# Packing one head group's q projection into pad rows, gathering it over DRAM, and laying the instruction order anew

## The chip, the cores and the metric

The kernel runs on one core of a Trainium2 chip. The metric is device time in microseconds (us), the median of several executions. The trace gives a span that is some 1.8 us shorter (182.2 us of span is 183.97 us of time in the profiled run of the kernel before). Ratios below are the mean time of one kernel's fast runs over that of the other's fast runs of the same rounds, so they are not quite the ratios of the medians that are quoted. "Clock" is the granted clock of TensorE in the records, 1.00 being full.

The kernel before was run again beside every experiment on the same chip. Its medians then lay between 184.4 and 185.2 us, single executions between 184.0 and 187.0 (and one of 441, an outlier), so differences under 0.3% are read with care. The record marks an execution as slow when it is over 1.5% above the fastest of the same kernel; such executions are left out of every ratio quoted here.

## The reference

Two branches are mixed by a gate for each token. S = 2048 tokens, D = 448, H = 16 heads of 28, four segments of 512 tokens, F = 1792.

```
g = sigmoid(sum(x * gate_w))
q, k, v = heads(x @ wq), heads(x @ wk), heads(x @ wv)
for s in 4 segments:                               # attention with a compressive memory
    a_dot = softmax(causal(q_s k_s^T / sqrt(28))) v_s
    a_mem = phi(q_s) M / (phi(q_s) z + 1e-6)       # phi(t) = t+1 if t>0 else exp(t)
    o_s   = sigmoid(beta) * a_mem + (1 - sigmoid(beta)) * a_dot
    M, z += phi(k_s)^T v_s, sum phi(k_s)
a = o @ wo
b = (gelu(layernorm(x)^T @ w1 + b1) @ w2 + b2)^T   # mixes tokens: w1 is 2048 x 1792
out = g * a + (1 - g) * b
```

## The kernel before

All five engines follow one fixed list of steps, `PLAN`. Each entry names a step and its engine (`@P` TensorE, `@A` ScalarE, `@D` VectorE, `@G` GpSimd, `@S` SyncE, which issues DMAs); digits after it are buffers. Each engine works through its own entries strictly in this order and waits on semaphores for the others. So the list decides what TensorE does while ScalarE works on exponentials.

Four heads of 28 form a group of 128 partitions, each head with four pad rows. A k/q projection is a `pair`: k in the lower, q in the upper half of the array, 14 matmuls. With four groups (`hg`) and four token chunks (`tc`) there are 16 pairs:

```
def pair(eng, u, tc, hg):
    ...
        for i in range(7):
            for h, c, bb in ((0, LC[i], bk), (1, UC[i], bq)):
                last = e.matmul(bank(bb)[:, 0:512], wkq[half[h], c, 128*hg : 128*hg+128],
                                xTb[half[h], b, i, :], start=(i == 0), stop=(i == 6), ...)
def ek(...): copy k out of its PSUM bank        # eviction; eq the same for q
def sc(...): scores of one of five groups of tiles of two head groups   (TensorE)
def exp(...): exponential of 128x2048           (ScalarE)
def mask(...): causal mask                      (GpSimd)
def pv(...): P times V                          (TensorE)
def ta, tm, nr, oa, om, oo, ot: normalize one of 16 items, memory and local part  (VectorE)
def mm_u, eu / mm_y, fin: the two MLP products and their evictions / last additions
```

Part of the list around 46 us, which this document comes back to: the pair of the last head group of chunk 2 stands between two score groups.

```
... u.2.7@P mask.1.2@G u.2.8@P ot.1@D sc.1.3@P ek.2.2@A
pair.2.3@P01 xtc.3@S oa.0@D1 exp.1.3@A2 ot.0@D ldr.2@S2 pv.2@P31 eq.2.3@D ek.2.3@A mask.1.3@G sc.1.4@P ...
```

The softmax here doesn't subtract the row's maximum and nothing guards it: scores larger than these inputs give would overflow.

Of the kernel before, what the change touches and what calls it, by code (L numbers as in the profile page):

```python
# [4 lines left out]
ALU = mybir.AluOpType  # L5
# [16 lines left out]
NO = 3  # L22
# [11 lines left out]
warm@P ldwk.0@A dve0@D id@G ldx.0@S ldx.1@S ldwq.0@A setup@G ldsm@S ldwv.0@A ldwv.1@A acttab@A ldwk.1@S ldwq.1@S  # L34
trx.0.2@P xw.0@D xtd.1@S trx.0.3@P trx.0.0@P trx.0.1@P trx.0.6@P trx.0.4@P trx.0.5@P trx.1.2@P xw.1@D trx.1.3@P
trx.1.0@P trx.1.1@P ex.1@A trx.1.6@P trx.1.4@P ex.0@D trx.1.5@P ex.2@D ex.3@A pad.0@D tb@A bn.3@D pair.0.0@P01 bn.0@D
bet@D btr@P2 eq.0.0@A ek.0.0@A pair.0.1@P31 b2c@D pad.1@A gcp@D b1c@D bn.1@D bn.2@D sc.0.0@P xtc.1@S v.1@P02 ek.0.1@D
lnc.0@G exp.0.0@A0 eq.0.1@D ldx.2@S pkm.0.0@D0 pair.0.3@P31 ldr.0@S0 ev.2@D pke.0.0@A0 ev.3@D sc.0.1@P gt.1@A
pkn.0.0@D eq.0.3@A pair.0.2@P02 exp.0.1@A1 ek.0.3@D pair.1.0@P13 ldx.3@S bn.5@D eq.0.2@A bn.4@D mask.0.0@G xtd.2@S
ek.0.2@A lna.0@D mask.0.1@G sc.0.2@P lna.1@A bn.6@D pair.1.3@P20 eq.1.0@A pkm.0.1@D1 lna.2@A bn.7@D pke.0.1@A1  # L40
ek.1.0@D lnc.1@G eq.1.3@D pair.1.1@P31 exp.0.2@A2 ek.1.3@D pkn.0.1@D v.3@P02 lna.3@D eq.1.1@A bn.11@D ek.1.1@A bn.9@D
sc.0.3@P mask.0.2@G ev.6@A v.0@P13 ev.7@D ldx.4@S lna.4@A bn.10@D gt.3@A exp.0.3@A3 pkt.0.0@S0 bn.8@D pair.1.2@P02
ev.0@D lnc.2@G ev.1@D pkt.0.2@S lna.7@A lna.6@D sc.0.4@P gt.0@A ek.1.2@D eq.1.2@A pv.0@P10 lna.5@A bn.15@D xtc.2@S
v.2@P32 exp.0.4@A0 pqm.1.1@D0 bn.14@D ldr.1@S1 bn.12@D mask.0.3@G u.0.0@P0 bn.13@D u.0.1@P u.0.2@P ev.5@A u.0.3@P
mask.0.4@G gc.0@D u.0.4@P ev.4@A u.0.5@P lna.8@D u.0.6@P u.0.7@P lna.9@A sc.1.0@P pqm.1.0@D1 lnc.3@G u.0.8@P pkt.0.3@S
gt.2@A lna.10@D pqe.1.1@A0 u.0.9@P u.1.0@P2 gc.1@D u.1.1@P u.1.2@P lna.11@D u.1.3@P pqe.1.0@A1 pv.1@P31 pqn.1.1@D
pkt.0.1@S u.0.10@P exp.1.0@A1 ta.0@D u.0.11@P u.1.4@P u.1.5@P pqn.1.0@D u.1.6@P u.1.7@P xtd.3@S u.1.8@P u.1.9@P
pkm.1.0@D1 u.1.10@P u.1.11@P lna.15@D lna.12@A sc.1.1@P mask.1.0@G nr.0@D lna.14@A mst.0@P1 pkm.1.1@D0 lna.13@D
exp.1.1@A5 ta.1@D u.1.12@P u.1.13@P u.1.14@P msa.0@D u.1.15@P u.0.12@P u.0.13@P eu.1@D u.0.14@P pke.1.1@A0 mask.1.1@G
sc.1.2@P nr.1@D pair.2.2@P31 msc.0@D pke.1.0@A1 oa.1@D0 exp.1.2@A0 pkn.1.1@D u.2.0@P2 u.2.1@P u.2.2@P pkn.1.0@D  # L50
u.2.3@P ldwo@S u.0.15@P u.2.4@P u.2.5@P eu.0@D u.2.6@P eq.2.2@A u.2.7@P mask.1.2@G u.2.8@P ot.1@D sc.1.3@P ek.2.2@A
pair.2.3@P01 xtc.3@S oa.0@D1 exp.1.3@A2 ot.0@D ldr.2@S2 pv.2@P31 eq.2.3@D ek.2.3@A mask.1.3@G sc.1.4@P ta.2@D u.3.0@P1
exp.1.4@A3 mem.4@P00 u.2.9@P pqm.2.1@D2 mem.5@P31 tm.4@D u.2.10@P pkt.1.0@S1 u.2.11@P u.2.12@P u.2.13@P tm.5@D
u.2.14@P u.2.15@P pqe.2.1@A0 u.3.1@P nr.2@D mask.1.4@G u.3.2@P eu.2@D sc.2.0@P pkt.1.1@S pair.3.3@P03 oa.2@D2
exp.2.0@A1 pqn.2.1@D ldr.3@S0 ot.2@D pv.3@P20 ek.3.3@A eq.3.3@D mask.2.0@G sc.2.1@P u.3.3@P ta.3@D exp.2.1@A5 u.4.0@P0
u.3.4@P u.4.1@P pkt.1.2@S pkm.2.1@D1 u.4.2@P u.4.3@P nr.3@D u.4.4@P u.3.5@P oa.3@D0 u.3.6@P v.7@P32 pke.2.1@A1
mask.2.1@G pkt.1.3@S ot.3@D pkn.2.1@D sc.2.2@P ev.15@A u.3.7@P u.3.8@P ev.14@D exp.2.2@A0 u.3.9@P u.3.10@P u.3.11@P
u.3.12@P u.3.13@P u.3.14@P u.3.15@P u.4.5@P u.4.6@P eu.3@D ldr.4@S1 gt.7@A u.4.7@P mask.2.2@G u.4.8@P u.4.9@P wo.0@P20
u.5.0@P3 u.5.1@P ea.0@A u.5.2@P u.5.3@P wo.1@P11 wo.2@P22 ea.1@D sc.2.3@P ea.2@A pv.4@P11 exp.2.3@A2 u.4.10@P ta.4@D
u.4.11@P u.4.12@P u.4.13@P u.4.14@P nr.4@D u.4.15@P v.6@P21 eu.4@D mask.2.3@G oa.4@D1 sc.2.4@P om.4@D ev.13@A wo.3@P03  # L60
exp.2.4@A3 ev.12@D u.5.4@P oo.4@D u.5.5@P u.5.6@P ea.3@D u.5.7@P u.5.8@P u.5.9@P u.5.10@P ot.4@D gt.6@A u.5.11@P
mask.2.4@G u.5.12@P u.5.13@P gc.3@D u.5.14@P u.5.15@P pair.3.2@P01 eu.5@A ldr.5@S2 pv.5@P20 eq.3.2@A mem.6@P30
ek.3.2@A pqm.3.1@D3 mst.1@P1 ta.5@D pqe.3.1@A0 tm.6@D sc.3.0@P v.5@P02 exp.3.0@A1 nr.5@D msa.1@D oa.5@D2 u.6.0@P3
u.6.1@P u.6.2@P ev.10@D u.6.3@P mask.3.0@G sc.3.1@P om.5@D u.6.4@P exp.3.1@A5 u.6.5@P u.6.6@P ev.11@D mem.7@P11
u.6.7@P oo.5@D u.6.8@P u.6.9@P tm.7@D u.6.10@P u.6.11@P u.6.12@P gt.5@A u.6.13@P pqn.3.1@D mask.3.1@G sc.3.2@P v.4@P10
exp.3.2@A0 msc.1@D ot.5@D u.6.14@P ev.8@D u.6.15@P u.7.0@P2 u.7.1@P eu.6@A mask.3.2@G ev.9@D sc.3.3@P u.7.2@P gelu.0@A
u.8.0@P3 u.8.1@P u.8.2@P u.8.3@P u.8.4@P u.8.5@P u.8.6@P u.8.7@P u.8.8@P u.8.9@P u.8.10@P u.8.11@P u.8.12@P u.8.13@P
u.8.14@P u.8.15@P u.7.3@P u.7.4@P eu.8@D u.7.5@P u.7.6@P u.7.7@P u.7.8@P pv.6@P31 u.7.9@P ta.6@D u.7.10@P u.7.11@P
gt.4@A exp.3.3@A2 u.7.12@P gc.2@D pair.3.0@P01 nr.6@D oa.6@D0 u.7.13@P mask.3.3@G om.6@D eq.3.0@A u.7.14@P u.7.15@P
sc.3.4@P ek.3.0@A eu.7@D ldr.6@S0 pair.2.0@P31 exp.3.4@A3 oo.6@D ot.6@D pair.2.1@P02 ek.2.0@D eq.2.0@A mask.3.4@G  # L70
sc.4.0@P ek.2.1@A eq.2.1@D pv.7@P30 exp.4.0@A1 pkm.2.0@D0 pair.3.1@P10 ta.7@D pqm.2.0@D1 nr.7@D pke.2.0@A1 u.9.0@P2
mask.4.0@G eq.3.1@D u.10.0@P3 u.10.1@P u.10.2@P oa.7@D1 u.10.3@P pqe.2.0@A0 u.10.4@P u.10.5@P u.9.1@P pqm.3.0@D0
sc.4.1@P om.7@D u.10.6@P exp.4.1@A5 u.10.7@P u.10.8@P pqn.2.0@D u.10.9@P u.10.10@P u.10.11@P u.10.12@P oo.7@D
u.10.13@P u.10.14@P pkn.2.0@D u.10.15@P mem.8@P00 pqe.3.0@A0 mask.4.1@G sc.4.2@P eu.10@D pkt.2.0@S0 u.9.2@P u.9.3@P
tm.8@D exp.4.2@A6 u.9.4@P u.11.0@P3 u.11.1@P u.11.2@P pqn.3.0@D u.11.3@P u.11.4@P pkt.2.2@S u.11.5@P ot.7@D u.11.6@P
u.11.7@P u.11.8@P u.11.9@P mask.4.2@G ek.3.1@D sc.4.3@P u.11.10@P pkt.2.1@S exp.4.3@A0 u.11.11@P u.11.12@P u.11.13@P
u.11.14@P pv.8@P01 u.11.15@P pkt.2.3@S ta.8@D mem.9@P11 mask.4.3@G sc.4.4@P u.9.5@P eu.11@D exp.4.4@A2 u.9.6@P u.9.7@P
nr.8@D u.9.8@P ldr.7@S2 u.12.0@P0 tm.9@D u.12.1@P u.9.9@P u.9.10@P u.9.11@P oa.8@D2 u.12.2@P u.12.3@P mask.4.4@G
u.12.4@P sc.5.0@P om.8@D u.12.5@P exp.5.0@A3 u.12.6@P u.12.7@P oo.8@D mem.10@P30 u.12.8@P ot.8@D u.12.9@P u.12.10@P
u.12.11@P u.12.12@P tm.10@D u.12.13@P u.12.14@P mask.5.0@G u.12.15@P sc.5.1@P eu.12@D u.9.12@P exp.5.1@A4 u.9.13@P  # L80
# [166 lines left out]
def build_kernel(nc, X, WQ, WK, WV, WO, BETA, W1, B1, W2, B2, GW, OUT):  # L247
# [130 lines left out]
    def ldwk(eng, u, j):  # L378
        ldw_half(eng, WK, 0, j, R_wk[j])
# [609 lines left out]
```

## Time and profile before

| | before |
|---|---|
| time, median of 3 | 184.34 us |
| span of the profiled run, clock | 182.2 us, 1.00 |
| TensorE busy / idle | 172.7 / 9.5 us |
| VectorE, ScalarE, GpSimd busy | 135.7, 123.9, 54.5 us |
| matmuls of k/q pairs | 224 (16 x 14) |

The prediction shows the busy shares and the stretches up to 42 us. It joined all from 42 to 151 us in one line, in which TensorE is busy throughout. Cut finer, the same view shows what that line hides. The columns are the stretch, its length, busy time of TensorE, its weight loads, VectorE, ScalarE and GpSimd (instructions in brackets), clock, DMA share and GB/s.

```profile
42.00:60.00 18.00, 18.00 (x172) 7.63 (x165) 16.28 (x28) 16.96 (x16) 5.70 (x7) 1.00 0.89 177
60.00:80.00 20.00, 20.00 (x185) 9.22 (x185) 14.42 (x29) 12.49 (x15) 4.21 (x5) 1.00 0.39 106
80.00:100.00 20.00, 20.00 (x175) 8.47 (x172) 14.87 (x30) 18.56 (x16) 4.01 (x5) 1.00 0.20 54
116.00:151.00 35.00, 35.00 (x291) 16.48 (x289) 26.46 (x47) 26.65 (x17) 11.15 (x11) 1.00 0.48 139
```

TensorE is full in all four, but its company is not the same. Up to 60 us ScalarE (16.96 of 18) and VectorE (16.28 of 18) are full as well. From 60 to 80 us they work 12.49 and 14.42 of 20 us. What a removed pair is worth turned out to depend on this.

The chain that ended last, by engine, is TensorE for three quarters:

```profile
PE 75%; SPq 6%; DVE 6%; ACT 5%; DMA 4%; POOL 1%; issue 1%
```

### The profile page before, as it was taken

Reading aid. Unit: us, or ns where it says so; the run is one execution under the profiler, and the core shown is the slowest. Engines: PE = TensorE matmul, PEld = TensorE weight load, DVE = VectorE, ACT = ScalarE, POOL = GpSimd, SP = SyncE. Lnnn points to the kernel's source line nnn. Section 1 sums busy time; section 2 is a strip of 40 time slices with the busy share of each in tenths; the row PEclk is TensorE's granted clock in tenths of the full one; section 3 lists DMA queues with packets and bytes.
Section 4 is the critical chain, followed back from the end, with each engine's and each line's share of the span. In section 5 each row is a group of like instructions: output and inputs, shape, how many; then the busy total and the mean of one; then the engine's idle time right before and its main releaser. Section 6 shows DMA issues by size and latency. Waiting matters only on the chain.

```text
span 182.2 us, 3611 instructions
## 1 busy us (share of the span) xinstructions
PE 172.7 (95%) x1471; PEld 79.7 (44%) x1471; DVE 135.7 (74%) x268; ACT 123.9 (68%) x116; POOL 54.5 (30%) x89
## 2 busy tenths in 40 slices
PE   7568999999999999999999999999999999999994
PEld 2323334353444444544344444644444444455553
DVE  5659799989997385993779676199895937997322
ACT  2458999999999375789989868997747677000100
POOL 8006487752332212141121431401343441300000
DMA  6995999997993621600080452760074560088012
GB/s 156 219 196 148 320 178 213 281 168 181 249 231 83 177 53 48 185 0 0 4 227 9 86 163 69 225 181 25 29 227 128 173 206 0 28 249 229 27 39 63
DMA packets 50368, 24.92 MB, mean 137 GB/s; under 512 B 15088, under 2 KB 49968, under 8 KB 50352
## 3 DMA queue, kind: packets, MB, share of 16 engines
q1 hardware_dynamic: 48496, 23.44, 54.3%
q10 hardware_dynamic: 1856, 1.26, 3.4%
q8 instruction: 11, 0.18, 0.5%
q14 instruction: 5, 0.04, 0.1%
HBM read 18.54 MB, written 1.84 MB: 112 GB/s over the span
## 4 chain that ended last, share of the span: by engine, by line
PE 75%; SPq 6%; DVE 6%; ACT 5%; DMA 4%; POOL 1%; issue 1%
PE t L902 22%; PE t L849 21%; PE t L545 8%; PE t L875 7%; PE t L694 6%; SPq L356 6%; PE t L570 5%; PE t L735 4%; DMA t<-in_A_x_dram 4%; ACT t L704 3%; ACT t L835 2%; PE t L748 2%; PE t L659 1%; DVE t L366 1%; DVE t L803 1%
## 5 line engine op out<-in xcount | busy, mean ns | idle before, releaser
L704 ACT ACTIVATE t<-t 128x2048 bf16<-128x2048 f32 x40 | 75.1, 1878 | 14.4 <-PE t L694 14.3
L717 POOL TENSOR_SCALAR_AFFINE_SELECT t<-t 128x1024 bf16<-128x1024 bf16 (+1 forms) x40 | 38.2, 956 | 86.0 <-ACT t L704 78.6
L849 PE MATMUL t<-t 128*128 128x448 bf16 x224 | 47.9, 354 | 0.2
L902 PE MATMUL t<-t 128*128 128x448 bf16 (+1 forms) x238 | 46.2, 342 | 0.1
L902 PEld LDWEIGHTS t<-t 128*128 128x128 bf16 x238 | 22.7, 98 | 19.6 <-issue 1.5
L849 PEld LDWEIGHTS t<-t 128*128 128x128 bf16 x224 | 20.2, 98 | 22.5 <-issue 5.0
L545 PE MATMUL t<-t 64*128 64x512 bf16 x224 | 26.6, 377 | 3.3 <-DVE t L366 2.8
L364 ACT ACTIVATE t<-t 128x512 bf16<-128x512 f32 (+4 forms) x27 | 16.4, 644 | 5.0 <-PE t L545 2.2
L911 DVE SCALAR_TENSOR_TENSOR t<-t 128x448 bf16<-128x448 f32 (+1 forms) x17 | 11.0, 647 | 11.3 <-PE t L902 11.3
L545 PEld LDWEIGHTS t<-t 64*128 64x128 bf16 x224 | 9.8, 94 | 16.9 <-DVE t L366 3.9
L694 PE MATMUL t<-t 28*128 28x512 bf16 (+3 forms) x256 | 15.8, 301 | 0.3 <-ACT t L704 0.3
L366 DVE CAST t<-t 128x512 bf16<-128x512 f32 (+1 forms) x24 | 15.1, 647 | 1.1 <-PE t L545 0.8
L885 ACT ACTIVATE t<-t 128x448 bf16<-128x448 f32 x4 | 2.9, 724 | 18.9 <-PE t L875 18.9
L755 DVE STREAM_TRANSPOSE t<-t 128x512 f32<-128x512 f32 x16 | 11.3, 709 | 5.0 <-PE t L735 5.0
L875 PE MATMUL t<-t 128*128 128x448 bf16 x64 | 14.1, 353 | 0.0
L888 DVE TENSOR_SCALAR t<-t 128x448 bf16<-128x448 f32 x12 | 8.7, 728 | 6.3 <-PE t L875 6.3
L613 ACT ACTIVATE t<-t 128x1024 bf16<-128x1024 bf16 x12 | 12.4, 1064 | 0.0
L570 PE MATMUL t<-t 64*128 64x449 bf16 x112 | 12.0, 350 | 0.0
L735 PE MATMUL t<-t 128*32 128x512 bf16 (+3 forms) x256 | 11.3, 301 | 0.4 <-ACT t L590 0.4
L795 DVE STREAM_TRANSPOSE t<-t 128x512 bf16<-128x512 bf16 x16 | 11.0, 691 | 0.2
L784 DVE TENSOR_TENSOR t<-t 128x448 bf16<-128x448 f32 x12 | 10.9, 911 | 0.1
L776 DVE SCALAR_TENSOR_TENSOR t<-t 128x448 bf16<-128x448 f32 x16 | 10.9, 687 | 0.1
(67 smaller groups left out, 149.3 us busy)
## 6 DMA issues: line engine op xcount, KB each, us to landing
t<-in_B_w_dram SPq DMA_DIRECT2D x7, 1024.0 KB, 7.6
t<-in_B_w_dram SPq DMA_DIRECT2D x8, 896.0 KB, 5.5
out_dram<-t SPq DMA_DIRECT2D x15, 112.0 KB, 1.7
t<-in_A_x_dram SPq DMA_DIRECT2D x3, 448.0 KB, 4.7
t<-t SPq DMA_DIRECT2D x6, 192.0 KB, 3.0
t<-in_A_wv_dram ACTq DMA_DIRECT2D x2, 392.0 KB, 6.9
t<-in_A_x_dram SPq DMA_DIRECT2D x2, 224.0 KB, 3.6
t<-in_A_wo_dram SPq DMA_DIRECT2D x4, 98.0 KB
```

The lines of the kernel that those rows point to most:

```text
L364: op("ACT", lambda e: e.activation(out, in_, ACT.Copy), reads=reads, writes=writes)
L366: op(eng, lambda e: e.tensor_copy(out, in_), reads=reads, writes=writes)
L545: last = e.matmul(bank(bb)[:, 0:512], wkq[half[h], c, 128 * hg : 128 * hg + 128], xTb[half[h], b, i, :], start=(i == 0), stop=(i == 6), sk ...
L570: last = e.matmul(bank(bs[h])[:, 0 : D + 1], xTb[half[h], b, i, k0 : k0 + 128], wvx[half[h], (LC, UC)[h][i], 0 : D + 1], start=(i == 0), s ...
L613: op("ACT", lambda e: e.activation(et[:, i, :].rearrange("p (g t) -> p g t", g=2), two(T, hp, s), ACT.Exp), reads=[RT[2 * hp][s], RT[2 * h ...
L694: last = e.matmul(bank(hl)[:, c0 : c0 + w], kT[r, hg, s * 512 + j * 128 : s * 512 + j * 128 + 128], qT[r, hg, s * 512 + 128 * j : s * 512 ...
L704: op("ACT", lambda e: e.activation(punit(i).rearrange("p (a q) -> p a q", a=4), ps[:, 0:4, :], ACT.Exp, scale=SCALE), reads=R_bank[0:4], w ...
L717: op("POOL", lambda e: e.affine_select(d, d, pattern=pat, compare_op=ALU.is_ge, fill=0.0, base=0, channel_multiplier=-1), reads=[R_P[i]], ...
L735: last = e.matmul(bank(b)[32 * hl : 32 * hl + 32, 128 * j : 512], vaug[:, 4 * s + j, 32 * h : 32 * h + 32], p4[:, hl, c0 : c0 + w], start= ...
L849: op("PE", lambda e: e.matmul(bank(b)[:, 0:D], w[:, st, (ft % 2) * 128 : (ft % 2) * 128 + 128], xtile(st)[:, 0, :], start=(st == 0), stop= ...
L875: last = e.matmul(bank(b)[:, 0:D], oT[:, hg, T * 128 : T * 128 + 128], wo_sb[:, hg, :], start=(hg == 0), stop=(hg == NHG - 1), skip_group_ ...
L902: op("PE", lambda e, b=b, f=f, c0=c0, n=n: e.matmul(bank(b)[:, 0:n], w[:, f, c : c + 128], uT[:, f, c0 : c0 + n], start=(f == 0), stop=(f ...
```

## The change

Its intent: the q features of the last head group (heads 12 to 15) are worked out in the four pad rows of each head slot of the seven other k and q groups, at no cost in matmuls. Then only k of that group has to be computed, two chunks at a time (`pair3`): 14 pairs instead of 16. The pad rows are brought together by a write to DRAM and a read back. The weights of wq for the pads (`rider`) must be there before the first pair, so wq is loaded first and whole; the V weights go behind x on SyncE's queue. The memory and local normalization become one instruction. The list is laid out anew.

```diff
-def pair(...): 14 matmuls, k and q of group hg           # 16 times
+def two_products(jobs): 14 matmuls, two products of any kind
+def pair(...):  k and q of group hg, hg = 0..2           # 12 times
+def pair3(...): k of group 3 for chunks tc and tc + 1    # 2 times
+def rider(...): q weights of heads 12..15 into pad columns of a weight block   # 8 copies
+def gw(eng, u, tc):     # all 128 rows of seven groups to DRAM, 918 kB a chunk
+    dma(eng, scr[tc, :, 0:4, :], kT[:, :, s], ...)
+    dma(eng, scr[tc, :, 4:7, :], qT[:, 0:3, s], ...)
+def gr(eng, u, tc):     # the pad rows back, as q of group 3
+    for hl in range(4):
+        src = scr[tc, 32*hl + DH : 32*hl + 32, :, :].rearrange("r g t -> (r g) t")
+        dma(eng, qT[32*hl : 32*hl + DH, 3, 512*tc : 512*tc + 512], src, ...)
...
-oa: scalar_tensor_tensor 128x448;  om: tensor_tensor 128x448
+oa: tensor_tensor 128x896 (both parts);  nr: one multiply of 16 columns more
...
-warm@P ldwk.0@A dve0@D id@G ldx.0@S ldx.1@S ldwq.0@A ... ldwv.0@A ldwv.1@A acttab@A ldwk.1@S ldwq.1@S
+warm@P ldwq@A dve0@D id@G ldx.0@S ldx.1@S ldwk.0@A setup@G ldwk.1@S ldsm@A ldwv.0@S ldwv.1@S xtd.1@S acttab@A
... (all of PLAN in another order)
```

## The prediction

> **What bounds the kernel now.** I read the page's busy shares first, then the slices, then busy time by stretches, to see where TensorE is not full.
>
> ```profile
> PE 172.7 (95%) x1471; PEld 79.7 (44%) x1471; DVE 135.7 (74%) x268; ACT 123.9 (68%) x116; POOL 54.5 (30%) x89
> ...
> PE   7568999999999999999999999999999999999994
> ...
> DMA  6995999997993621600080452760074560088012
> ```
> ```profile
> 4.50:10.00 5.50, 3.47 (x43) 2.04 (x40) 3.08 (x7) 2.07 (x4) 0.00 (x0) 1.00 1.18 215
> 10.00:16.00 6.00, 3.74 (x35) 1.43 (x37) 4.56 (x22) 5.04 (x6) 0.87 (x5) 1.00 0.85 152
> 16.00:24.00 8.00, 7.66 (x78) 2.98 (x80) 7.04 (x14) 7.09 (x12) 4.65 (x13) 1.00 1.12 283
> 24.00:32.00 8.00, 7.63 (x91) 3.35 (x89) 7.87 (x16) 8.00 (x14) 6.51 (x18) 1.00 1.09 188
> 32.00:42.00 10.00, 9.50 (x89) 4.36 (x85) 9.24 (x24) 9.84 (x12) 5.92 (x14) 1.00 1.19 220
> 42.00:151.00 109.00, 109.00 (x937) 48.74 (x930) 81.97 (x148) 87.35 (x70) 30.72 (x32) 1.00 0.48 122
> ```
>
> In the second fence the columns are the stretch, its length, busy time of TensorE, its weight loads, VectorE, ScalarE and GpSimd, then granted clock, DMA share, GB/s. TensorE has no gap at all in the 109 us from 42 to 151 us. Of the span of 182.2 it idles 9.5: 1.3 before 4.5 us, 2.0 + 2.3 up to 16 us, 0.3 + 0.4 + 0.5 up to 42, 0.1 in 151 to 158, and 2.5 at the end (the last addition and store). So a matmul taken away anywhere is worth its time, if the early gaps don't grow. From 16 to 42 us, VectorE (24.2 of 26 us), ScalarE (24.9) and the DMA engines are full too: there is no slack for added work there.
>
> The start, in order of time on TensorE:
>
> ```profile
> 5.67 0.95 PE L517 MATMUL t<-t 128*128 128x128 bf16 x14 [0.34 <-DMA t<-in_A_x_dram]
> 8.21 1.69 PE L545 MATMUL t<-t 64*128 64x512 bf16 x14 [1.58 <-DVE t L366]
> ...
> 11.55 1.68 PE L545 MATMUL t<-t 64*128 64x512 bf16 x14 [0.54 <-ACT t L364]
> 13.17 0.39 PE L694 MATMUL t<-t 28*128 28x512 bf16 x4
> 13.59 1.50 PE L570 MATMUL t<-t 64*128 64x449 bf16 x14
> 15.96 0.61 PE L545 MATMUL t<-t 64*128 64x512 bf16 x4 [0.87 <-DVE t L366]
> ```
>
> The second half of x lands at about 5.65; its transposes take 0.95; copies to SBUF and the padding of the weights follow on VectorE; the first k/q projection (L545) starts at 8.21. Each bracket is a wait on the chain.
>
> **What the Trainium skill says.** "TensorEngine Tiling (Array Packing)", section "Tiling Modes", has a 2x row tiling of 64 rows each whose tiles run in parallel. The trace agrees: one matmul of L545 has a mean of 377 ns, but 14 take 1.62 us from one group to the next, 116 ns each. "DMA: Bandwidth & Descriptors", section "Issuing engines are not separate DMA queues", says that DMAs of all issuers share the same 16 engines, and a second issuer only saves issue time. So moving the V weights to another queue changes an order, not a bandwidth; the DMA line, full from the second slice on, fits. "SBUF — State Buffer", section "Who interferes with whom", says that a VectorE instruction with two SBUF inputs contends with a GpSimd one that reads SBUF. This fits the first group below, whose single instructions last 562 to 1519 ns; the 1519 one ran beside a mask on GpSimd.
>
> ```profile
> L784 DVE TENSOR_TENSOR t<-t 128x448 bf16<-128x448 f32 x12 | 10.9, 911 | 0.1
> L776 DVE SCALAR_TENSOR_TENSOR t<-t 128x448 bf16<-128x448 f32 x16 | 10.9, 687 | 0.1
> ```
>
> **The change, part by part.** (1) Projections. Before: 4 chunks x 4 groups = 16 pairs of 14 matmuls. After: 12 pairs plus 2 double ones, which compute the last k group for two chunks at once = 14. Two pairs go: 2 x 1.62 = **3.24 us off TensorE**. The q values of the last four heads come for free in the four pad columns of each head slot. Four evictions of about 0.62 us go too (2.5 us of ScalarE and VectorE together); eight small copies that place these columns come (estimate 0.2 to 0.3 each, 2 us): even, but the copies stand at the very start.
>
> (2) Start. The copies read only wq, now one load of 401 kB, first on ScalarE's queue, with half of wk behind. Before the padding 459 (x) + 401 + 229 + 172 (wk) = 1261 kB must move. The page moves 710 kB in the first 4.55 us and then 219 GB/s: 551 / 219 = 2.5, so 7.1 us, and with about 0.8 of completion 7.9. wq by the same count (equal shares for both queues) is there at about 5.8. On VectorE four copies (0.8) now stand before the two small copies of x that the transposes need: transposes end at about 7.8 in place of 6.6. Then a copy (0.69), the padding (0.7) and another copy (0.69), one behind the other: the first pair starts at about 9.6, **1.4 us later**. The V weights' move doesn't change this, since the bytes before the padding are no fewer than now.
>
> (3) Up to 18 us. Three pairs now run back to back, 9.6 to 14.5. Next is the double pair, which needs x's second chunk. That comes by DMA transpose and a copy: now landed at 14.0, copies issued 14.0 and 14.6, 3.0 to land, 17.6. The same bytes lie ahead of it after the change, so I put it at 17.2: a gap of 2.7, as much as the present gaps from 9.9 to 16 (0.93 + 0.54 + 0.87 and crumbs). Up to the third V pair I count by order 6 pairs, 3 V products and 2 score groups, with a 0.9 us wait for the first exponential, done at 27.9. The kernel before has by 28.1 done 7 pairs, 3 V products, 4 score groups. In TensorE time 9.7 + 4.3 + 0.7 = 14.7 against 11.3 + 4.3 + 1.3 = 17.0: behind by 2.3 - 0.2 = 2.1 us, of the 3.24 gained. Part of this is the delayed start, the rest is waiting; I take 1.7, since the larger rows of wq could bring everything a little forward.
>
> (4) The gather. Each chunk writes 128 x 7 KB = 918 kB to DRAM and reads 115 kB back; four are 4.1 MB on 24.9. Three come after 50 us, where DMA has room. The first stands in SP's order ahead of the third chunk's copy and of the second W1 load, while DMA is full: 918 / 220 GB/s = 4.2 us later, less one transposing load (about 1.2) that now comes behind: 3. The second W1 load lands now at about 37.6 to 38.8 (issued 29.99, 7.6 to land); after, 40 to 41.5. The third chunk's copy goes from about 33 to 36. In the new order its first user, a pair behind 18 + 5 first-MLP matmuls, is due at about 33.3 (27.9 + 23 x 0.19 + a wait for the second exponential), and the W1 user at 39 to 42. **A wait of 0 to 2.7 us; I take 1.0.** The later rest of the early gaps (0.7 now) I put 0.3 smaller.
>
> (5) Norms fused. Twelve times 687 + 911 ns become one tensor_tensor of 896 elements and a 16-column multiply (0.15, as L769). From the shortest, 562 ns for 448 elements at 1.04 ns each, the fused one takes 1.03 undisturbed; GpSimd adds 0.35 on average now (911 - 562), and at least that to a longer one: 1.4 to 1.65 + 0.15 against 1.60. Nothing gained, up to 2 us lost on VectorE, beside matmuls: 0 on the end.
>
> Sum: 182.2 - 3.24 + 1.7 + 1.0 - 0.3 = 181.4 us of span. A run is timed 1.8 to 2.2 us above it (183.97 with the profile, median 184.34): about **183.3**. I lower this to **182.8**, because the new order was evidently laid out anew for these waits and my hand count may see more of them than there are.
>
> **Rivals.** First: the whole gain arrives. Then the early wait only changes its place, the first gather is hidden behind other loads, and the time is 184.34 - 3.24 = 181.1, or 180.5 with shorter gaps. For it: after 42 us nothing but TensorE counts. Against it: a later first pair by VectorE's own order, and a full DMA in the same stretch. Second: the gather's traffic becomes the bound from 30 to 45 us; waits of 3 us or more for the second W1 load or third chunk give 184.5 to 186. For it: DMA at nine tenths for twelve slices. Against: 23 first-MLP matmuls were put in front. Third: the attention blocks come late, since exponentials start later; ScalarE or VectorE would leave gaps after 60 us. Against: in 158 to 182 us ScalarE works only 0.7 us, so 1 to 2 us of delay find room; +0 to 1.5.
>
> **Range and chances.** The sure part is -3.24; the doubts are 1 to 2 us at the start and 0 to 3 at the gather. Predicted 182.8, range 180.4 to 185.0. Two per cent faster is below 180.65, which needs all of the gain and a shorter start: 0.15. Above 188 would need several new waits: 0.03. Within: 0.82.
>
> **What would show it.** Right: 196 projection matmuls and TensorE busy down by 3.2 to about 169.5; the first pair at 9 to 10 us; a wait for DMA before the double pair near 17; TensorE idle at least 10 us, the new part of it before 45; the fused instruction at 1.3 to 1.7 us. Wrong: a first pair at 8.2 or earlier, or no wait for DMA from 14 to 45 us (then nearer 181); or gaps of several us after 60 us, of which my reading has none (then above 185).

## The result, and the profile after

The changed kernel took 189.96 us (188.98 to 190.66, 4 fast runs) against 184.42 us (184.3 to 186.0, 4 runs) for the kernel before: ratio 1.0276, 95% interval 1.0204 to 1.0349, slower. The predicted 182.8 us was wrong in its sign. The profiled run has a span of 188.1 us, 5.9 more than before, at a mean clock of 0.991.

The page of the changed kernel, busy shares, TensorE's slices and the clock's slices:

```profile
PE 171.7 (91%) x1437; PEld 79.7 (42%) x1443; DVE 137.4 (73%) x266; ACT 128.2 (68%) x127; POOL 54.8 (29%) x90
...
PE   7475999889999999998999998999996999999994
...
PEclk9999699999999999999999999999999999999999
```

TensorE has 28 fewer weight loads (1443 after, 1471 before): the two pairs. (The page lists 34 fewer matmuls; six more are missing from this trace, since each matmul has its weight load.) Yet it is busy only 1.0 us less, and it idles 188.1 - 171.7 = 16.4 us instead of 9.5. The chain that ended last now runs over VectorE for a quarter:

```profile
PE 44%; DVE 27%; DMA 12%; SPq 10%; ACT 2%; issue 2%; POOL 2%; DVEq 0%
```

Where the idle time lies, by the same stretches as in the prediction and above:

```profile
4.50:10.00 5.50, 2.35 (x29) 1.80 (x27) 2.98 (x10) 4.76 (x9) 1.72 (x1) 1.00 1.18 204
10.00:16.00 6.00, 4.88 (x43) 2.09 (x43) 5.12 (x21) 3.54 (x7) 2.81 (x10) 1.00 0.87 154
16.00:24.00 8.00, 5.99 (x46) 2.92 (x46) 5.04 (x13) 4.11 (x9) 0.85 (x4) 0.79 1.15 294
...
60.00:80.00 20.00, 19.65 (x170) 8.77 (x168) 14.38 (x26) 17.26 (x18) 5.90 (x6) 1.00 0.47 121
80.00:100.00 20.00, 19.20 (x201) 8.60 (x201) 16.77 (x30) 16.72 (x14) 6.58 (x7) 1.00 0.49 146
...
116.00:151.00 35.00, 32.77 (x293) 15.40 (x294) 29.94 (x52) 26.15 (x18) 8.73 (x9) 1.00 0.35 100
```

Summed over all stretches, TensorE idles 9.4 us up to 60 us (before 6.8), 4.4 from 60 to 158 (before 0.1) and 2.6 at the end (before 2.5). In 16 to 24 us the clock is 0.79. From 116 to 151 us VectorE works 29.94 of 35 us, 3.5 more than before.

The waits of TensorE that stand behind these sums, in order of time; the bracket is the idle time ahead of the group and what ended it:

```profile
10.24 3.20 PE L558 MATMUL t<-t 64*128 64x512 bf16 x28 [1.64 <-DVE t L367]
...
18.01 2.37 PE L558 MATMUL t<-t 64*128 64x512 bf16 x14 [2.32 <-DMA t<-t]
...
86.30 0.92 PE L891 MATMUL t<-t 128*128 128x448 bf16 x4 [0.64 <-DVE t L902]
...
114.47 0.55 PE L891 MATMUL t<-t 128*128 128x448 bf16 x2 [0.75 <-DVE t L902]
...
129.15 0.73 PE L944 MATMUL t<-t 128*128 128x448 bf16 x3 [0.41 <-DVE t L953]
...
143.11 0.73 PE L776 MATMUL t<-t 128*32 128x512 bf16 x16 [1.56 <-DVE t L953]
```

The first pair starts at 10.24 us (before 8.21), the double pair waits 2.32 us for x's second chunk. It then takes 2.37 us for 14 matmuls instead of 1.69. The later waits are for VectorE: L902 evicts the first MLP product, L953 is the last addition, and both free the PSUM bank that the next matmul writes.

So the balance of the spans is: -3.24 for the pairs; +2.2 because the remaining matmuls ran longer (171.7 is not 172.7 - 3.24 = 169.5); +2.6 idle up to 60 us; +4.3 from 60 to 158 us; together +5.9. The balance says where, not why. One of the prediction's own signs of being wrong is in it: "gaps of several us after 60 us, of which my reading has none (then above 185)". Three suspects are the gather, the new order, and the loads and norms.

### The profile page after: what moved, and what is told of

Read it like the earlier page. It is cut to its first block, busy times and chain, and to the rows that moved or that the text cites. A ratio compares the mean times of both kernels' runs of the same rounds, so it can differ in the third digit from the quotient of the medians.

```text
span 188.1 us, 3587 instructions
## 1 busy us (share of the span) xinstructions
PE 171.7 (91%) x1437; PEld 79.7 (42%) x1443; DVE 137.4 (73%) x266; ACT 128.2 (68%) x127; POOL 54.8 (29%) x90
## 4 chain that ended last, share of the span: by engine, by line
PE 44%; DVE 27%; DMA 12%; SPq 10%; ACT 2%; issue 2%; POOL 2%; DVEq 0%
PE t L944 16%; PE t L891 12%; SPq L357 10%; DMA t<-t 8%; DVE t L828 5%; PE t L917 4%; DVE t L796 3%; PE t L558 3%; PE t L611 3%; PE t L735 3%; PE t L776 3%; DMA t<-riders 2%; DMA t<-in_A_x_dram 2%; DVE t L800 2%; DVE t L834 2%
## 5 line engine op out<-in xcount | busy, mean ns | idle before, releaser
L758 POOL TENSOR_SCALAR_AFFINE_SELECT t<-t 128x1024 bf16<-128x1024 bf16 (+1 forms) x40 | 37.4, 937 | 89.8 <-ACT t L745 84.5
L558 PE MATMUL t<-t 64*128 64x512 bf16 x196 | 23.9, 385 | 5.0 <-DMA t<-t 2.3
L365 ACT ACTIVATE t<-t 128x512 bf16<-128x512 f32 (+6 forms) x33 | 18.5, 593 | 6.8 <-PE t L558 3.7
L953 DVE SCALAR_TENSOR_TENSOR t<-t 128x448 bf16<-128x448 f32 (+1 forms) x17 | 10.9, 641 | 10.4 <-PE t L944 10.4
L735 PE MATMUL t<-t 28*128 28x512 bf16 (+3 forms) x256 | 15.8, 301 | 0.5 <-ACT t L745 0.5
L558 PEld LDWEIGHTS t<-t 64*128 64x128 bf16 x196 | 9.0, 95 | 16.9 <-issue 3.0
L828 DVE TENSOR_TENSOR t<-t 128x896 bf16<-128x896 f32 x12 | 15.3, 1280 | 0.2
L367 DVE CAST t<-t 128x512 bf16<-128x512 f32 (+1 forms) x20 | 13.0, 658 | 3.0 <-PE t L558 2.3
L927 ACT ACTIVATE t<-t 128x448 bf16<-128x448 f32 x8 | 5.7, 725 | 13.8 <-PE t L917 13.8
L611 PE MATMUL t<-t 64*128 64x449 bf16 x112 | 12.9, 373 | 0.0
L658 DVE TENSOR_TENSOR t<-t 128x1024 bf16<-128x1024 bf16 x12 | 9.0, 747 | 4.6 <-ACT t L654 4.6
L845 DVE BATCH_NORM_STATS2 t<-t 128x6 f32<-128x448 bf16 x16 | 9.0, 612 | 2.8 <-DMA t<-in_A_x_dram 2.8
```

Source lines behind the costliest of these rows:

```text
L365: op("ACT", lambda e: e.activation(out, in_, ACT.Copy), reads=reads, writes=writes)
L558: last = e.matmul(bank(bb)[:, 0:512], wkq[half[h], c, 128 * blk : 128 * blk + 128], xTb[half[h], b, i, :], start=(i == 0), stop=(i == 6), ...
L611: last = e.matmul(bank(bs[h])[:, 0 : D + 1], xTb[half[h], b, i, k0 : k0 + 128], wvx[half[h], (LC, UC)[h][i], 0 : D + 1], start=(i == 0), s ...
L735: last = e.matmul(bank(hl)[:, c0 : c0 + w], kT[r, hg, s * 512 + j * 128 : s * 512 + j * 128 + 128], qT[r, hg, s * 512 + 128 * j : s * 512 ...
L758: op("POOL", lambda e: e.affine_select(d, d, pattern=pat, compare_op=ALU.is_ge, fill=0.0, base=0, channel_multiplier=-1), reads=[R_P[i]], ...
L828: op("DVE", lambda e: e.tensor_tensor(out, both, rec[:, a, :, :, None].to_broadcast([128, 2, 16, DH]), op=ALU.mult), reads=[R_tA[a], R_tM[ ...
```

## The experiments

Eighteen kernels ran. All passed the comparison with the reference, also the four that were wrong on purpose. The inputs are 0.05 times a normal variable and the weights smaller still, so wrong attention presumably moves the output by less than the tolerance. The comparison therefore does not show that the gathered q values are right. A functional simulation, which is not among the recorded runs, used x 20 times and wq and wk 60 times larger: the changed kernel and the gather kernels below agree with the kernel before to one bf16 step (0.004), and the kernel with two pairs left out differs by 1.2.

### One part undone or done alone

**Ten dummy matmuls ahead of the double pair**, in the changed kernel, to take the gap before it and its low clock away:

```diff
-... btr@P3 eq.0.2@A ...
+... btr@P3 gapfill.10@P eq.0.2@A ...
```

> The changed kernel with ten matmuls of zeros put into TensorE's gap of 2.3 us before the first double pair (15.7 to 18.0 us), into a PSUM bank that is free. Theory clock: the long gap lowers TensorE's granted clock afterwards (the double pair takes 2.37 us in place of 1.69), and filling it gives a granted clock of 1.00 from 16 to 24 us, the pair in 1.69, and the V products 1.5 us earlier; of these about 2 us, 1 to 2 reach the end (188 to 189 us). Rival: the low clock has another cause than the gap; then the clock stays at 0.8 in that stretch and the time at 190.

Measured: 189.72 us (189.15 to 190.52), ratio 1.025, not clearly apart from the changed kernel. The gap is filled, but in this run the lowered clock sat one stretch earlier:

```profile
10.00:16.00 6.00, 5.59 (x40) 2.19 (x42) 4.58 (x18) 3.66 (x6) 2.71 (x10) 0.72 0.86 158
16.00:24.00 8.00, 7.93 (x67) 3.25 (x65) 6.10 (x18) 4.97 (x11) 0.92 (x5) 1.00 1.13 293
```

TensorE works 7.93 of 8 us in 16 to 24 us, instead of 5.99 (2.3 us of it are the dummies), and the later waits are where they were. The first single pair behind the V products started at 23.63 us, 0.67 earlier than in the changed kernel; but the third exponential ended at 36.2 us, against 36.0, so other waits had taken the lead away within 12 us. One execution at a recorded mean clock of 1.00 took 190.52.

**All three early waits filled**, the last run of the study, set here because it belongs to this one: six dummies behind the first transposes, seven ahead of the first pair, ten ahead of the double pair.

```diff
-... trx.0.5@P trx.1.2@P ... trx.1.5@P pad.0@D ... pair.0.1@P01 ... btr@P3 ...
+... trx.0.5@P gapfill.6@P trx.1.2@P ... gapfill.7@P pair.0.1@P01 ... btr@P3 gapfill.10@P ...
```

> The changed kernel with dummy matmuls in all three early waits of TensorE: six behind the first transposes, seven ahead of the first pair, ten ahead of the double pair, none of which can end after the wait that it fills. In the changed kernel the real matmuls are busy 171.7 us, 2.2 more than the 169.5 that they take at full clock. If the early low clock is part of what the new order costs: first pairs at 1.62 us for 14 matmuls, no stretch below 0.9 of clock, busy time about 169.5 plus 5 for the dummies, time 187.5 to 188.5. If it is not on the path to the end (a run at a recorded 1.00 took 190.5): 189.5 to 190.3.

Measured: 190.71 us (189.92 to 191.99), ratio 1.0306. This run went partly wrong: the dummies took longer than the waits, and the first pair came 2.9 us later than in the changed kernel, at 13.12 us, the double pair at 20.05 instead of 18.01. In return all pairs ran at full clock, so that at the pair behind the V products only 0.35 us of the delay was left. This run, then the changed kernel:

```profile
13.12 4.71 PE L573 MATMUL t<-t 64*128 64x512 bf16 x42
...
24.65 1.69 PE L573 MATMUL t<-t 64*128 64x512 bf16 x14
```

```profile
24.30 1.69 PE L558 MATMUL t<-t 64*128 64x512 bf16 x14
```

The low clock is thus worth some 1.7 us up to there (2.04 of delay less 0.35). But by the run before this one, even a lead at 24 us is gone by 36, so no run shows that it counts at the end.

**The gather out, all else as changed**: direct pairs, no pad columns, no DRAM traffic, but the loads, norms and order of the changed kernel.

```diff
-rider.*  gw.*  gr.*  pair3.0  pair3.2
+pair.0.3 pair.1.3 pair.2.3 pair.3.3  (with eq.*.3), in the places of the double pairs
```

> The changed kernel with the last q group projected directly again (two pairs in place of each double pair, 3.24 us more on TensorE), without the eight column copies, the DRAM writes and the reads; order, loads and fused norms as changed. Theory gather: the latency and traffic of the gather cause the late attention and most of TensorE's new gaps (6.97 us), so the time falls in spite of the added matmuls, to 185 to 187. Rival order: the late start, the clock and the new order as such cause them; then the 3.24 us come back on top of 190: 191 to 193.

Measured: 194.14 us (193.18 to 194.88), ratio 1.0499. Without its gather the changed kernel is 4.2 us slower still. The theory that the gather's traffic or its waits cost the time fell here; inside its own order the gather, with its two pairs less, gains 4.2 us.

**The fused norms alone**, in the kernel before:

```diff
-oa.N@D (local part)  om.N@D (memory part)       # N = 4 to 15
+oa.N@D (both parts), nr.N@D with one multiply more
```

> The kernel before with only the norms fused (one instruction for 687 + 911 ns, plus a 16-column multiply), in its own order. Theory: fusing is nearly free for VectorE (1.28 + 0.2 us in the changed kernel against 1.60), so 184.0 to 184.8. Rival: the longer instruction holds up VectorE where its order is tight (near 152 us), so 185 to 187.

Measured: 185.47 us (185.1 to 186.73), ratio 1.0026 (1.0002 to 1.0049): a quarter of a per cent, some 0.5 us, to the bad.

**The loads alone**, in the kernel before (its load entries replaced by those of the diff above):

```diff
-warm@P ldwk.0@A ... ldwq.0@A setup@G ldsm@S ldwv.0@A ldwv.1@A acttab@A ldwk.1@S ldwq.1@S
+warm@P ldwq@A ... ldwk.0@A setup@G ldwk.1@S ldsm@A ldwv.0@S ldwv.1@S acttab@A
```

> The kernel before with only the loads of the changed kernel: wq whole and first on ScalarE's queue, then half of wk, the small vectors there too; the other half of wk and the V weights on SP's queue behind x. Theory loads: the padding now needs 1261 kB in place of about 917, so the first pair starts 1 to 1.5 us later than 8.2 and the time is 184.5 to 185.5. Rival: it is the column copies, not the loads, that made the first pair late (10.2 us); then the first pair stays at 8.2 to 8.6 and the time at 184.0 to 184.5.

Measured: 186.28 us (185.9 to 186.89), ratio 1.0083: 1.5 us. The first pair started at 9.20 us instead of 8.21 and took 3.17 us instead of 1.69. So a whole wq ahead of the padding moved the first pair by 1.0 us, and its matmuls then ran slower by 1.5 us. A recorded mean clock of 0.99 came in 14 of these 17 executions, but in only 4 of 28 of the kernel before; at equal recorded clock the loads cost 0.8 us (0.99) to 1.3 us (1.00).

**The order alone**: the kernel before with its own instructions, loads and norms and all 16 pairs, in the new order.

```diff
-PLAN of the kernel before
+PLAN of the changed kernel without rider, gw, gr, pair3; with pair.0.3 to pair.3.3, om.N and the loads of before
```

> The kernel before (all 16 pairs, separate norms, old loads) with its instructions put into the order of the changed kernel: no part of the change but the order. Theory order: the new order as such costs most of the loss, since without the gather the changed kernel took 194.1 us; then 191 to 194, with TensorE gaps of 3 to 5 us between 60 and 151 us. Rival: the parts (copies and loads at the start, fused norms) make the new order fail; then 184 to 187.

Measured: 194.49 us (193.13 to 194.95), ratio 1.049. The new order by itself costs 9 us. Its profiled span of 192.6 us has 7.2 us more idle time of TensorE than before, in eighteen waits of up to 3.1 us, and 3.2 us more busy time at a clock of 0.982. Three stretches of this run, with the columns as above:

```profile
10.00:16.00 6.00, 2.91 (x24) 1.19 (x22) 2.61 (x16) 2.59 (x4) 2.81 (x10) 0.92 0.85 152
16.00:24.00 8.00, 6.43 (x37) 2.51 (x35) 4.75 (x12) 3.51 (x6) 0.00 (x0) 0.63 1.15 290
...
116.00:151.00 35.00, 33.00 (x287) 15.27 (x289) 27.78 (x51) 27.42 (x21) 9.47 (x11) 1.00 0.42 119
```

Summed like the balance above, the order alone adds 2.4 us of idle up to 60 us, 4.9 from 60 to 158 us and 3.2 of slower matmuls. The changed kernel adds 2.6, 4.3 and 2.2. So all three losses are there without gather, new loads or fused norms. The changed kernel wins back 4 to 5 us by its other parts. (This order was laid out for 14 pairs; with 16 it may do worse than it must.)

**The gather alone, in the old order**: pad rows only written (115 kB a chunk), the old loads as far as possible.

```diff
-pair.0.3 pair.1.3 pair.2.3 pair.3.3 (eq.N.3 with them)
+rider.* (ScalarE, VectorE)  pair3.0 pair3.2  gw.0 to gw.3  gr.0 to gr.3
-dma(eng, scr[tc, :, 0:4, :], ...)  dma(eng, scr[tc, :, 4:7, :], ...)
+for hl in range(4): dma(eng, scr[tc, 32*hl+DH : 32*hl+32], kq[32*hl+DH : 32*hl+32, 0:7, s], ...)
```

> Only the gather, in the order of the kernel before: double pairs where the pairs of the last group stood, loads as before except that the last columns of wq come first, separate norms, and only the pad rows written to DRAM (115 kB a chunk in place of 918). Theory order: the two pairs saved show up, less 0.5 at the start: 181 to 183. Rival gather: the added latency of q makes this one slower too, 185 to 188.

Measured: 191.44 us in the one fast execution; three of four were in the slow state, so there is no ratio. Far above both expectations. In its trace SyncE was held for 3.27 us by the four reads of the first gather, ahead of the transposes of the keys' features; VectorE then waited 3.47 us for these, and TensorE 2.64 us for VectorE at 42.35 us. That was my own placing, so the run says nothing of the gather.

### Repairs of the new order, and of the gather in the old one

**Four VectorE instructions moved ahead** in the changed kernel, those that released TensorE late:

```diff
-oo.10@D y.3.11@P y.3.12@P oa.11@D2 y.3.13@P ... y.4.4@P fin.3@D
+y.3.11@P y.3.12@P y.3.13@P fin.3@D oo.10@D oa.11@D2 ... y.4.4@P
 (fin.0 ahead of ot.8, eu.7 ahead of oa.5, eu.11 ahead of pqn.3.1 likewise)
```

> The changed kernel with four VectorE instructions moved ahead of others in its static order, nothing else: two evictions of the first MLP product ahead of the fused normalization (they released TensorE at 86.3 and 114.5 us after 0.64 and 0.75 us of idle) and two final additions ahead of normalization work (129.2 and 143.1 us, 0.41 and 1.56 us). If TensorE's late idle time is a matter of which VectorE instruction stands first at those four places, three of those gaps go, TensorE idles about 2.5 us less between 60 and 151 us, and the time comes down from 190.0 to 187 to 188. Rival, VectorE simply has too much work left in that stretch because the attention began late: the gaps come back at the next wait on VectorE, within 10 us, and the time stays at 189.3 to 190.

Measured: 189.42 us, ratio 1.0244 (1.0222 to 1.0266), 0.3% below the changed kernel's. Its profiled run fell in the slow state, so its waits are not compared. Its time lies where the rival put it: moving what stands first gained nothing that the runs resolve. That the gaps came back elsewhere is not shown.

**The first five score groups one place earlier**, in the changed kernel, the first of them in the gap ahead of the double pair:

```diff
-btr@P3 ... pair3.0@P02 ... sc.0.0@P ... sc.0.1@P ... sc.0.2@P ...
+btr@P3 ... sc.0.0@P pair3.0@P02 ... sc.0.1@P ... sc.0.2@P ...   (exp and mask with them)
```

> The changed kernel with the five score groups of the first two head groups, their exponentials and masks each one place earlier, the first group ahead of the double pair, where TensorE waited 2.32 us for the x chunk. If the late start of the attention (first exponential at 24.5 us, 13.6 us before) makes the later waits: first exponential at 17.8 us, gap before the double pair about 1.9 us, time 188 to 189.3. If the late start is repaid later anyway or the later waits have another cause: 189.5 to 190.3.

Measured: 190.25 us (189.78 to 190.62), ratio 1.0293. The first exponential ended at 21.3 us instead of 26.4, and nothing came of it: the sixth ended at 50.0 us, against 48.9 in the changed kernel. **Both repairs at once:**

```diff
+ both diffs above
```

> The changed kernel with both earlier repairs of its order at once: the four VectorE instructions moved ahead and the first five score groups one place earlier. Alone they made 189.4 and 190.3 of 190.0 us. If each hid the other's gain (late attention fed the late VectorE work): 187 to 188.5. If the cost of the new order is spread over its length and not in these places: 189 to 190, ratio 1.023 to 1.028.

Measured: 191.79 us, but from 189.04 to 193.19, two of four executions in the slow state: inconclusive. The two fast ones took 189.04 and 190.75, so there is no sign that the two hid each other's gain.

**Half of the gather, in the old order**: chunks 0 and 1 keep their direct pairs, chunks 2 and 3 are gathered; one pair goes. Weights for the pads are copied on GpSimd.

```diff
-pair.2.3@P01 (at 46 us) ... pair.3.3@P03 (at 51 us)
+(nothing)               ... pair3.2@P03
```

> The kernel before in its own order, with its own loads and norms, but with the gather for the last two token chunks only: chunks 0 and 1 keep their direct projections, one pair of 14 matmuls goes (1.62 us), the pad columns are copied into the weights on GpSimd between 5 and 28 us, only the pad rows are written to DRAM. Here nothing of the start is touched, no load is moved, and the gather has tens of us before it is needed. If the idea of the change is sound and only its order and start cost time: 182.6 to 184.0 against 184.8 for before, ratio 0.990 to 0.997, TensorE idle within 1 us of the 9.5 us before. If a gather costs what it gains wherever it stands: 184.5 to 187, with new TensorE idle of 1 to 3 us after 90 us.

Measured: 189.46 us (189.18 to 189.78), ratio 1.0252, with a profiled clock of 1.00. This is above both expectations: 5 us lost, although all pairs at the start were left as they stood. At 46 us TensorE now waited 0.47 us for the mask and 0.85 for the exponential; between 112 and 136 us it waited four times for VectorE, 3.8 us together, in a stretch where the kernel before has no gap. **And the whole gather in the old order, mended:**

```diff
-ldr.1@S1 gr.0@S ... pkt.0.1@S       rider.*@A, @D    gr.2@S pkt.2.0@S0
+ldr.1@S1 ... pkt.0.1@S gr.0@S       rider.*@G        pkt.2.3@S gr.2@S
 (chunk 2's pairs ahead of chunk 3's)
```

> The run with the gather alone in the order of before, mended: the read of chunk 0 behind the transposes of the keys' features on the queue of SyncE (it held them up by 3.3 us, and TensorE with them by 2.64 us at 42.35), the pad copies on GpSimd rather than on ScalarE and VectorE, chunk 2's projections ahead of chunk 3's so that its gather has time. If that queue order was what made the run slow: no gap over 1 us between 32 and 60 us, no lowered clock there, 183 to 186. If the gather of four chunks costs more than 3.24 us even so, through the loads at the start and waits at 118 to 142 us: 187 to 191.

Measured: 193.74 us (fast runs 192.72 to 194.13), ratio 1.0462, above both expectations too. Its profiled clock is 1.00:

```profile
PE 169.5 (89%) x1434; PEld 78.8 (41%) x1443; DVE 134.7 (70%) x268; ACT 122.7 (64%) x115; POOL 58.5 (31%) x98
```

172.7 - 169.5 = 3.2 us: the matmuls went, to the last tenth. But the span of 191.5 us has 22.0 us of idle time in it, 12.5 more than before. Not all of this is the place of the removed pairs: the first pair waited 2.41 us for the weight copies on GpSimd, and from 72 to 140 us five waits for VectorE sum to 6.1 us. So the gather in the old order brought waits of its own.

### What is a removed pair worth?

The question had become simpler than the change. **Two early pairs left out of the kernel before**, nothing else touched; the evictions copy what stands in the banks (wrong on purpose).

```diff
 def pair(eng, u, tc, hg):
     ...
+    if (tc, hg) in ((1, 3), (2, 3)):
+        return
```

> The kernel before with the matmuls of two of its sixteen pairs simply left out (the last head group of chunks 1 and 2), every other instruction in its place; the evictions copy what stands in the banks, so the result is wrong on purpose. It measures what the removal is worth where no gather and no other order stands against it. If 28 matmuls less are 3.24 us less, as the prediction took it: span 179, time 181 to 181.8, ratio 0.981 to 0.985. If the pairs were filling time in which the scores, exponentials and masks set the pace, so that leaving them out only opens holes: TensorE busy 3.2 us less, idle 2 to 3 us more at 24 to 60 us, time 183.5 to 185.

Measured: 186.18 us (184.26 to 187.64, 20 runs), ratio 1.0046 (1.0017 to 1.0074). Taking 3.24 us of matmuls out gained nothing; it cost 0.4%. The same place on TensorE, first before, then with the pair left out:

```profile
45.76 0.40 PE L694 MATMUL t<-t 28*128 28x512 bf16 x4
46.09 1.69 PE L545 MATMUL t<-t 64*128 64x512 bf16 x14
47.70 0.73 PE L735 MATMUL t<-t 128*32 128x512 bf16 x16
48.36 0.40 PE L694 MATMUL t<-t 28*128 28x128 bf16 x8
```

```profile
48.13 0.40 PE L696 MATMUL t<-t 28*128 28x512 bf16 x4
49.00 0.73 PE L737 MATMUL t<-t 128*32 128x512 bf16 x16 [0.47 <-POOL t L719]
50.58 0.40 PE L696 MATMUL t<-t 28*128 28x128 bf16 x8 [0.85 <-ACT t L706]
```

L694 and L696 are the score groups. Before, 2.60 us lie between their starts, with a pair (L545, 1.69 us) and a P times V (L735) inside. Without the pair 2.45 us lie between them: TensorE waits 0.47 us for the mask (GpSimd) and 0.85 us for the exponential (ScalarE). The pair was filling. The other removed pair left this:

```profile
23.88 3.01 PE L547 MATMUL t<-t 64*128 64x512 bf16 x14 [1.96 <-DVE t L366]
```

1.96 us of waiting for an eviction, and after it 14 matmuls in 3.01 us instead of 1.69, at a clock of 0.79 from 24 to 32 us. The 20 runs show what that is worth. At a clock of 1.00 they took 184.50 us in the mean (6 runs), and the kernel before beside them 184.70 (27 runs): 0.2 us gained of 3.24, with an uncertainty of some 0.3. At 0.99 they took 186.31 (13 runs) against 185.62 (11 runs). So the holes alone make the two pairs worth nearly nothing, and a low clock, recorded in 14 of these 20 runs but in only 11 of 38 of the kernel before, makes it a loss.

**One late pair left out**: 12 of the 14 matmuls of chunk 3's third group, at 70.5 us in the trace (the expectations say 67), where ScalarE and VectorE have slack.

```diff
-            for i in range(7):
+            n = 1 if (tc, hg) == (3, 2) else 7
+            for i in range(n):
```

> The kernel before with 12 of the 14 matmuls of one late pair left out (chunk 3, third head group, at 67 us; wrong result on purpose), all else in place: 1.39 us less of TensorE in a stretch in which it is busy without a break and ScalarE and VectorE have slack. If what a pair is worth depends on where it stands: the time falls by 1.0 to 1.4 us, ratio 0.992 to 0.995, idle between 60 and 151 us below 0.5 us. If no pair is worth anything, because VectorE or ScalarE pace the whole program: ratio 0.998 to 1.002, with about 1.4 us of new idle behind 67 us.

Measured: 183.91 us (183.06 to 185.19, 22 runs), ratio 0.9947 (0.9927 to 0.9968). 1.39 us of matmuls are worth 1.0 us here. Where the pair stands decides how much of it counts. One sign failed: less than 0.5 us of idle was expected between 60 and 151 us, and the profiled run, one of the slowest at 185.0 us, has 0.95.

**Is VectorE's load the late bound?** Normalization of the last eight items left out, in the changed kernel and, as control, in the kernel before (both wrong on purpose):

```diff
     slot["o", n] = o
+    if n >= 8:
+        return
```

> The changed kernel with the fused normalization of the last eight of its sixteen items left out (8 of 1.28 us, 10 us of VectorE; wrong result on purpose). If TensorE's late waits come from VectorE having too much left to do in its order: TensorE's idle time between 60 and 158 us falls from 4.4 to under 2 us and the time to 186 to 188. If they come from the order of scores and exponentials, not from VectorE's load: 189 to 190 and idle time as before. The next run takes the same away from the kernel before.

> The control for the run before it: the kernel before without the normalization (both multiplies, 1.60 us an item) of its last eight items, wrong result on purpose. TensorE idles only 0.1 us between 60 and 158 us, so VectorE should have nothing to give back: 183.8 to 184.8, ratio 0.995 to 1.000. If it gains over 1 us, VectorE was a bound in the kernel before as well and the comparison says nothing of the change.

Measured: changed kernel 188.93 us (188.47 to 189.53), ratio 1.0225; control 184.85 us, ratio 0.9986. TensorE's late waits in the changed kernel shrank where VectorE was relieved:

```profile
100.00:116.00 16.00, 14.59 (x96) 6.36 (x92) 10.03 (x20) 14.08 (x12) 2.82 (x3) 1.00 0.81 191
116.00:151.00 35.00, 34.67 (x314) 16.31 (x319) 25.52 (x54) 28.27 (x23) 9.76 (x11) 1.00 0.38 110
```

In 116 to 151 us TensorE idles 0.33 instead of 2.23 us. But the ratio fell by half a per cent only, and its interval overlaps with that of the changed kernel. So VectorE's load does cause the waits of that stretch. But from 60 to 158 us TensorE still idles 3.4 us (4.4 before, under 2 expected), since it idles more from 60 to 80 and from 100 to 116 us. In time, these waits are about 1 us of the 5.5 at most, which the runs do not resolve.

### A gather that empties the right place

**The half gather, placed by what was learnt**: chunk 2's first pair moves up into the place at 46 us with its evictions, so that nothing opens there, and the place at 70 us falls empty. The features of the gathered group are worked out where VectorE waited for TensorE anyway.

```diff
-ek.2.2@A xtc.3@S ... pair.2.0@P01 eu.5@A (70 us) ... pkt.2.3@S gr.2@S
+ek.2.2@A pair.2.0@P01 xtc.3@S ... eu.5@A          ... gr.2@S pkt.2.0@S0
```

> The half gather in the order of before once more, but with the removed pair taken out at another place: chunk 2's first pair moves up to 46 us, where the pair of the last head group stood between two score groups, with its evictions, so that nothing opens there; the place that falls empty is at 67 us, where ScalarE and VectorE are busy 12.5 and 14.4 of 20 us. The read of the gather stands ahead of the transposes, and the features of the gathered head group are worked out where VectorE waited for TensorE anyway. If removed matmuls are worth their time where the other engines have slack, and nothing where they set the pace: no idle over 0.3 us at 43 to 60 us, 182.6 to 184.0, ratio 0.988 to 0.997. If a gather costs its gain wherever it stands: 185 to 189 as the other three.

Measured: 184.71 us (183.63 to 186.19, 22 runs), ratio 0.9982 (0.9959 to 1.0005). The same half gather as the run with 189.46 us, 2.7% better by placing alone: of the pair, of the read and of the features, which were not moved one by one. In the profiles the hole at 46 us (1.3 us) is gone, and so are the four late waits for VectorE (3.8 us), so most of the 5 us is not the place of the pair. One thing that may have kept it from gaining more was a small copy. On GpSimd the copies of weights for the shared pair stood ahead of a layer-norm step; VectorE waited for that:

```profile
27.46 1.67 POOL L377 COPY t<-t 64x112 bf16<-64x112 bf16 x3
```

```profile
40.02 0.67 DVE L892 TENSOR_SCALAR t<-t 128x448 bf16<-128x448 bf16 x1 [0.92 <-POOL t L883]
```

**The same with five of these copies moved** to where GpSimd waited:

```diff
-lnc.1@G rider.0.3@G rider.1.3@G kk@G ... mask.1.0@G
+lnc.1@G ... mask.1.0@G rider.0.3@G rider.1.3@G kk@G
-rider.0.0@G rider.1.0@G rider.0.1@G rider.1.1@G lnc.0@G ... mask.0.1@G
+rider.0.1@G rider.1.1@G lnc.0@G ... mask.0.1@G rider.0.0@G rider.1.0@G
```

> The run before, with five of its weight copies moved on GpSimd and nothing else: the three copies for the shared pair from 27.46 us (where they held the fourth layer-norm step up by 1.67 us; VectorE then waited 0.92 us for it, and TensorE lost 0.75 us at 41 us) to behind the first mask of the second head groups, where GpSimd waited 2.74 us; two more from ahead of the first layer-norm step to behind the second mask. If those copies are what ate the removed pair: no idle at 40.9 and 41.5 us, 183.2 to 183.9, ratio 0.990 to 0.996. If the pair is paid back otherwise, for example at the end: 184.5 to 185 as the run before.

Measured: 183.96 us (182.96 to 184.9, 10 runs) against 184.94 us, ratio 0.9957 (0.993 to 0.9983). TensorE's waits at 40.9 and 41.5 us (0.51 and 0.24) are now one of 0.32, at 41.6. This version beats both kernels: 0.4% below the one before, all of its interval below 1, though by less than the 2% that count as faster. Its interval overlaps with that of the run before it, so the worth of the moved copies is not resolved by time.

## Why the prediction was wrong

**The step that failed** is in the first part: "So a matmul taken away anywhere is worth its time, if the early gaps don't grow." It was drawn from a TensorE without a gap from 42 to 151 us. A full engine is not yet the one that sets the pace. The step entered the sum twice: as "-3.24" at full worth, and as no cost at all for a new order of the instructions after 45 us.

The runs showed this in its place. First, in the old order the worth depends on the place: two early pairs out gained 0.2 us of 3.24 at full clock, 12 matmuls of a late pair out 1.0 of 1.39. At 46 us TensorE was full because the list put a pair into a wait for the mask and the exponential. Second, TensorE is full from 42 us on only in the order of the kernel before. The new order by itself costs 9 us, with 4.9 us of new idle time between 60 and 158 us. The changed kernel has 4.3 there. So as far as the runs show, its loss comes with this order, and not from its removed pairs: within the new order the gather, with its two pairs less, is worth 4.2 us. The old order is no better home for the whole gather: there it took 193.74 us. Why the new order leaves these waits is shown only in part (below).

It was not tried whether other work could have filled the hole at 46 us; on paper, no PSUM bank was free for first-MLP matmuls beyond about 51 us.

The Trainium skill has the general form of this: "Perfetto Trace Analysis", section "Optimization Strategy", says that a kernel can have several regimes with another most-contended engine in each. The traces fit in part: TensorE is busiest throughout, but ScalarE is nearly as full from 42 to 60 us (16.96 of 18 us) and not from 60 to 80 us (12.49 of 20). I had read the shares of both engines and taken them as a warning against added work only, not against the worth of removed work.

**Projections, "3.24 us off TensorE".** The count was right (196 matmuls in `pair` and `pair3` after, L558 x196), and another kernel with the two pairs less, at full clock, shows 169.5 us busy as predicted. The changed kernel showed 171.7, since matmuls ran slower, at a recorded clock of 0.79 from 16 to 24 us. I had not foreseen this. I doubt that it decides: with the first gap filled, a lead of 0.67 us at 24 us was gone by 36 us. No run shows the changed kernel with a full clock and an undelayed start, so this stays open for up to 1.7 us.

**Start, "1.4 us later".** The first pair stood at 10.24 us, 2.0 later, not 1.4. The mechanism was right: VectorE's four copies began when wq landed, at 6.11 us, and the remaining transposes waited for them until 7.43. The size was short by 0.6. In the old order the loads alone moved the first pair by 1.0 us. What they cost in the new order was not measured by itself.

**Up to 18 us, "a gap of 2.7".** The double pair waited 2.32 us until 18.01 us; predicted 17.2. The mechanism was right, but filling the gap gained nothing that the runs resolve.

**The gather, "a wait of 0 to 2.7 us; I take 1.0".** TensorE waited for no DMA between 18 and 60 us. VectorE waited 2.4 us for the last gather's read near 112 us, which I had not looked at, having thought the later ones safe. Taken out, with its two pairs put back, the kernel was slower by 4.2 us. The new idle time up to 60 us, 2.4 us in the sum and 2.6 measured, thus agrees partly by luck: this wait was in it and did not come.

**Norms, "1.4 to 1.65 + 0.15 against 1.60", "0 on the end".** The fused instruction has a mean of 1280 ns, below the range given for it, and the extra multiply one of 305 ns, twice the 0.15 (a median of 235 ns, and one that took 1079): 1.59 us, so the sum was right. On the end it cost 0.26% alone, small but not 0 (interval 0.02 to 0.49%).

**The lowering to 182.8** "because the new order was evidently laid out anew for these waits" was unfounded. The order alone costs 9 us. The third rival named the place (gaps after 60 us, ScalarE or VectorE) but gave it 0 to 1.5 us; there are 4.3 us of such idle time. What the new order costs in each place is only partly settled. Late VectorE load is about 1 us of the changed kernel's loss at most, by the run with less of it. Moving four VectorE instructions (0.3%), earlier scores and a filled gap at the start gained nothing that the runs resolve. Where the rest lies stays open: the trace of the order alone shows it spread over eighteen waits.

## What to carry to other kernels

A full engine may be full of filling. Before counting on removed work, ask what stands around it: if two instructions of other engines fix the distance between its neighbours, leaving it out opens a hole of the same length. A cheap test is to leave the work out, wrong result and all, before building what is to replace it. And when work can be removed in several places, remove it where the other engines have slack, and move what is left into the places that need filling.

## What the Trainium skill lacked or had wrong

- "TensorE: Matmul & The Clock Gate", section "Part 1: The HAM clock gate (the "warmup" mystery)", puts the half clock after at least one idle window of some 3.4 us. Here a gap of only 1.96 us was followed by 14 matmuls that took 3.01 instead of 1.69 us. The page says that the slow stretch varies from run to run; that agrees, as 6 of the 20 executions had a clock of 1.00. It calls the ramp's penalty under 1% of a typical span; executions with a mean clock of 0.99 took 1.0% longer (186.3 against 184.5 us).
- The same section warns that records of the clock in traces can be unreliable, but has no number for it. In the run with less normalization, 42 projection matmuls from 11.11 us took 7.66 us (182 ns each, instead of 116), while the clock of 10 to 16 us is recorded as 1.00. So a recorded clock of 1.00 is no proof of full speed.
- "Perfetto Trace Analysis", section "Optimization Strategies", asks to keep the matmul engine busy. It lacks that busy time can be mere filling: 3.24 us of matmuls taken out of a TensorE that was 95% busy were worth 0.2 us at 24 and 46 us, and 1.39 us of a pair at 70 us were worth 1.0.
- No page gives the time of a gather through DRAM: writes of 512 and 384 kB landed 4.5 and 5.4 us after their issue (medians of four), and one read waited 5.6 us for its write on the same queue, holding all that stood behind it.
- No page has the time of such a small strided copy as a whole: one of 64x112 elements took 0.26 us on VectorE (1.05 for four), 0.35 on ScalarE (1.41 for four) and 0.40 to 0.56 on GpSimd (3.23 for eight, 1.67 for three).
